# The last block's transposes moved from TensorE to DMA, and the last tile stored in two halves

## Chip, cores, metric

The kernel runs on one core of a Trainium2 chip. The metric is the device time of one execution in microseconds (us); a median is quoted with its lowest and highest run. A ratio between two kernels is the mean time of one kernel's fast runs over the mean of the other's fast runs of the same rounds, so it is not quite the ratio of the medians. A run is called slow when it is over 1.5% above the fastest of the same kernel.

## The reference, cut to what matters

```python
def reference(A_x, A_k_cache, A_v_cache, A_wq, A_wo, B_x, B_w_gate, B_w_up, B_w_down):
    x  = A_x                                   # 2048 x 640, bf16
    xn = layernorm(x)
    s  = attention(xn)      # 32 heads of 192, the last 512 cached keys, then @ wo (6144 x 640)
    g  = silu((silu(xn @ w_gate) * (xn @ w_up)) @ w_down)
    return x + s * g
```

## The kernel before

Heads go in 16 pairs, rows in four blocks of 512, that is 16 tiles of 128 rows. For each pair and block the kernel computes scores, exponentials, `P @ V` (in `pv`), a transpose of the result `O_b` to `OT_b`, and `OT_b @ wo`. The products with `wo` are summed over pairs in `sacc`, already multiplied by `g` and with `x` added. For the last pair, `wo_last` multiplies its product by `g2` (VectorE reads PSUM, writes `s_f`), adds `sacc` (GpSimd or VectorE), and the sum goes to HBM.

Everything that the change touches lies in the last 25 us, where only the last pair is left. `sc_tile()` and `mm_tile()` each rotate over two PSUM buffers. In the cut below, `...` marks what is left out, and the comments are added.

```python
    def pv(i, q2):                       # P @ V of two row tiles, normalised into O_b
        ...
        if (pr == last and b < NB - 1) or i == 0:
            nc.sync.dma_start_transpose(
                out=OT_b[:, 6 * q2 : 6 * q2 + 6, :],
                in_=O_b[:, 2 * q2 : 2 * q2 + 2, :, :].rearrange("p t h d -> p (t h d)"),
            )
        ...
    def transpose_o(i, qt):              # the last block of the last pair only
        trp = psum.tile([P, 3, P], bf, name="trp", tag="mm")
        o_f = Obs[i][:, qt, :, :].rearrange("p h d -> p (h d)")
        for j in range(3):
            nc.tensor.transpose(trp[:, j, :], o_f[:, j * P : (j + 1) * P], ident[:])
        nc.scalar.copy(OTs[i][:, 3 * qt : 3 * qt + 3, :], trp[:, :, :])

    def wo_last(b, qt, eng):
        i, t = last * NB + b, 4 * b + qt
        ob = xrs[t] if b < 2 else finp.tile([P, D], bf, name="ob", bufs=4)
        s_f = finp.tile([P, 2, HD], f32, name="s_f", bufs=3)
        halves = [slice(n * HD, (n + 1) * HD) for n in range(2)]
        split = b == NB - 1 and qt == 3                       # the very last tile
        sc = None if split else sc_tile()
        ps = [(mm_tile()[:, 0, :] if split else sc[:, n, :])[:, 0:HD] for n in range(2)]
        for n, cols in enumerate(halves):
            if late(i):                                       # blocks 2 and 3: 12 matmuls, else 6
                wo_mm(ps[n], i - NB, qt, n, end=False)
            wo_mm(ps[n], i, qt, n, first=not late(i))
            if split:
                nc.vector.tensor_tensor(s_f[:, n, :], ps[n], g2[:, t, cols], ALU.mult)
                nc.vector.tensor_tensor(ob[:, cols], s_f[:, n, :], sacc[:, t, cols], ALU.add)
        if not split:
            nc.vector.tensor_tensor(
                s_f[:], sc[:, :, 0:HD], g2[:, t, :].rearrange("p (n d) -> p n d", n=2), ALU.mult
            )
            eng.tensor_tensor(
                ob[:], s_f[:].rearrange("p n d -> p (n d)"), sacc[:, t, :], ALU.add
            )
        stores.append((t, ob))

    def store(left):                                          # all on SyncE's queue
        while len(stores) > left:
            t, ob = stores.pop(0)
            nc.sync.dma_start(out=out2[t * P : (t + 1) * P, :], in_=ob[:])
    ...
    i = last * NB
    V, G = nc.vector, nc.gpsimd
    for b in range(NB - 1):
        for q2 in range(2):
            pv(i + b, q2)
    for q2 in range(2):
        wo_last(0, 2 * q2, G)
        wo_last(0, 2 * q2 + 1, G)
        pv(i + 3, q2)
    for qt in range(4):                                       # "the loop", four turns
        wo_last(1, qt, G)
        store(3)
        wo_last(2, qt, V if qt % 2 else G)
        transpose_o(i + 3, qt)
    for qt in range(4):                                       # "block 3"
        store(2)
        wo_last(3, qt, V if qt else G)
    store(0)
```

Below, "(2,1)" means block 2, tile 1; its product is s_f(2,1) and its sum ob(2,1).

The softmax here doesn't subtract the row's maximum and nothing guards it: scores larger than these inputs give would overflow.

Of the kernel before, what the change touches and what calls it, by code (L numbers as in the profile page):

```python
# [10 lines left out]
ALU = mybir.AluOpType  # L11
# [4 lines left out]
def kernel(  # L16
# [13 lines left out]
    nc = tc.nc  # L30
    P = nc.NUM_PARTITIONS

    x2 = A_x.flatten_outer_dims()
    out2 = out.flatten_outer_dims()
# [10 lines left out]
    NB = Sq // 512  # L45
# [5 lines left out]
    HD = D // 2  # L51
    scale = float(Dh) ** -0.5
    EPS = 1e-5
    bf = dt.bfloat16
# [14 lines left out]
    psum = ctx.enter_context(tc.tile_pool(name="psum", bufs=2, space=bass.MemoryType.PSUM))  # L69

    def sc_tile():
        return psum.tile([P, 2, 512], f32, name="sc", tag="sc")

    def mm_tile():
        return psum.tile([P, 2, 512], f32, name="mm", tag="mm")
# [5 lines left out]
    g2 = res.tile([P, T, D], bf, name="g2")  # L81


    ident = consts.tile([P, P], bf, name="ident")
# [313 lines left out]
    sacc = sapool.tile([P, T, D], f32, name="sacc")  # L398

    NS = NPAIR * NB  # L400
    last = NPAIR - 1
    Ps, OTs, Obs, xrs = {}, {}, {}, {}
# [32 lines left out]
    def pv(i, q2):  # L435

        pr, b = divmod(i, NB)
        if q2 == 0:
            Obs[i] = opool.tile([P, 4, 2, Dh], bf, name="O_b")
            tag = "OT_l" if late(i) and pr < last else "OT_b"  # L440
            OTs[i] = otpool.tile([P, 12, P], bf, name=tag, tag=tag, bufs=2 if tag == "OT_l" else 3)
        O_b, OT_b = Obs[i], OTs[i]
        alone = i < 2 or (pr == last and b < NB - 1)
        acc = sc_tile() if alone and q2 and b < 2 else mm_tile()
        r = smpool.tile([P, 2, 2, 1], f32, name="r")
        for k in range(2):
            qt = 2 * q2 + k
            for h in range(2):
                for kc in range(KC):
                    nc.tensor.matmul(  # L450
                        acc[:, k, h * 256 : h * 256 + Dh + 1],
                        Ps[i][kc][:, h, qt * P : (qt + 1) * P], V_p[:, kc, h, 0 : Dh + 1],
                        start=(kc == 0), stop=(kc == KC - 1),
                    )
        a_v = acc[:, :, :].rearrange("p k (h c) -> p k h c", h=2)
        nc.vector.reciprocal(r[:], a_v[:, :, :, Dh : Dh + 1])  # L456
        for k in range(2):
            qt = 2 * q2 + k
            a_k = a_v[:, k, :, :]
            if k == 0 and alone:  # L460
                nc.vector.tensor_tensor(
                    O_b[:, qt, :, :], a_k[:, :, 0:Dh], r[:, k, :, :].to_broadcast([P, 2, Dh]),
                    ALU.mult,
                )
                continue
            for h in range(2):
                nc.scalar.activation(  # L467
                    O_b[:, qt, h, :], a_k[:, h, 0:Dh], ACT.Copy, scale=r[:, k, h, :]
                )
        if (pr == last and b < NB - 1) or i == 0:  # L470
            nc.sync.dma_start_transpose(
                out=OT_b[:, 6 * q2 : 6 * q2 + 6, :],
                in_=O_b[:, 2 * q2 : 2 * q2 + 2, :, :].rearrange("p t h d -> p (t h d)"),
            )
        elif pr < last and q2 == 1:
            nc.sync.dma_start_transpose(
                out=OT_b[:, :, :], in_=O_b[:, :, :, :].rearrange("p t h d -> p (t h d)")
            )

    def transpose_o(i, qt):  # L480
        trp = psum.tile([P, 3, P], bf, name="trp", tag="mm")
        o_f = Obs[i][:, qt, :, :].rearrange("p h d -> p (h d)")
        for j in range(3):
            nc.tensor.transpose(trp[:, j, :], o_f[:, j * P : (j + 1) * P], ident[:])
        nc.scalar.copy(OTs[i][:, 3 * qt : 3 * qt + 3, :], trp[:, :, :])

    def load_xr(t):
        xrs[t] = finp.tile([P, D], bf, name="x_r", bufs=8)
# [3 lines left out]
    def late(i):  # L492
        return i // NB >= NPAIR - 2 and i % NB >= 2

    def wo_mm(ps, i, qt, n, first=True, end=True):
        for j in range(3):
            nc.tensor.matmul(  # L497
                ps, OTs[i][:, 3 * qt + j, :], pairs[i // NB]["wo"][:, j, n * HD : (n + 1) * HD],
                start=(first and j == 0), stop=(end and j == 2),
            )  # L500
# [23 lines left out]
# [5 lines that stand above are left out]
        split = b == NB - 1 and qt == 3  # L529
# [3 lines that stand above are left out]
            if late(i):  # L533
                wo_mm(ps[n], i - NB, qt, n, end=False)
            wo_mm(ps[n], i, qt, n, first=not late(i))
            if split:
                nc.vector.tensor_tensor(s_f[:, n, :], ps[n], g2[:, t, cols], ALU.mult)
                nc.vector.tensor_tensor(ob[:, cols], s_f[:, n, :], sacc[:, t, cols], ALU.add)  # L538
        if not split:
            nc.vector.tensor_tensor(  # L540
                s_f[:], sc[:, :, 0:HD], g2[:, t, :].rearrange("p (n d) -> p n d", n=2), ALU.mult
            )
            eng.tensor_tensor(
                ob[:], s_f[:].rearrange("p n d -> p (n d)"), sacc[:, t, :], ALU.add
            )
        stores.append((t, ob))

    def store(left):
# [4 lines that stand above are left out]
    for pr in range(NPAIR):  # L553
        for b in range(NB):
            i = pr * NB + b
# [22 lines left out]
        for b in range(NB):  # L578
            i = pr * NB + b
            for q2 in range(2):  # L580
                pv(i, q2)
                if i >= 2:
                    wo_tile(i - 2, 2 * q2)
                    wo_tile(i - 2, 2 * q2 + 1)
            if b == 0 and pr + 2 < NPAIR:
                load_k(pr + 2)
            elif b == 1 and pr + 2 < NPAIR:
                load_wq(pr + 2)
            elif b == 2:
                load_wo(pr + 1)  # L590
# [9 lines that stand above are left out]
    for qt in range(4):  # L600
        wo_last(1, qt, G)
        store(3)
        wo_last(2, qt, V if qt % 2 else G)
        transpose_o(i + 3, qt)
    for qt in range(4):
        store(2)
        wo_last(3, qt, V if qt else G)
    store(0)


# [28 lines left out]
```

## Time and profile before

The kernel before takes 930.39 us (930.12 to 930.56, 3 runs). Its page gives the busy time of each engine and the chain of work that ended last, by engine:

```profile
PE 920.7 (99%) x8026; PEld 578.7 (62%) x8026; DVE 579.7 (62%) x846; ACT 476.2 (51%) x849; POOL 65.1 (7%) x57
...
PE 98%; DMA 1%; DVE 1%; ACT 0%; issue 0%; SPq 0%; DVEq 0%
```

The same chain in order of time, at the end of the same kernel (columns: start, length, what), seems to agree. It counts each group of three transposes with 0.17 us:

```profile
906.33 2.44 PE sc L497 x18
908.78 0.17 PE trp L484 x3
908.94 0.81 PE sc L497 x6
909.76 0.00 issue
909.76 1.79 PE sc L497 x12
...
917.27 3.27 PE sc L497 x24
...
920.64 0.84 DVE s_f L540
```

The timelines of VectorE and GpSimd in that stretch tell more. First VectorE of the kernel before (start, length, engine, line, operation, out<-in, shapes, number; in brackets the idle time before it and what ended it):

```profile
908.88 0.82 DVE L540 TENSOR_TENSOR s_f<-sc,g_76 128x640 f32<-128x640 f32 x1 [0.81 <-PE sc L497]
...
911.66 0.82 DVE L540 TENSOR_TENSOR s_f<-sc,g_76 128x640 f32<-128x640 f32 x1 [0.97 <-PE sc L497]
912.52 0.99 DVE L543 TENSOR_TENSOR ob<-s_f,sacc 128x640 bf16<-128x640 f32 x1
...
918.07 1.47 DVE L543 TENSOR_TENSOR ob<-s_f,sacc 128x640 bf16<-128x640 f32 x1
919.46 0.81 DVE L540 TENSOR_TENSOR s_f<-sc,g_76 128x640 f32<-128x640 f32 x1
920.64 0.82 DVE L540 TENSOR_TENSOR s_f<-sc,g_76 128x640 f32<-128x640 f32 x1 [0.36 <-PE sc L497]
921.50 1.08 DVE L543 TENSOR_TENSOR ob<-s_f,sacc 128x640 bf16<-128x640 f32 x1
...
923.34 0.83 DVE L543 TENSOR_TENSOR ob<-s_f,sacc 128x640 bf16<-128x640 f32 x1
...
925.53 0.49 DVE L538 TENSOR_TENSOR ob<-s_f,sacc 128x320 bf16<-128x320 f32 x1
```

And GpSimd of the kernel before:

```profile
909.79 1.54 POOL L543 TENSOR_TENSOR ob<-s_f,sacc 128x640 bf16<-128x640 f32 x1
911.29 1.54 POOL L543 TENSOR_TENSOR x_r<-s_f,sacc 128x640 bf16<-128x640 f32 x1
...
917.31 1.55 POOL L543 TENSOR_TENSOR x_r<-s_f,sacc 128x640 bf16<-128x640 f32 x1
920.35 1.54 POOL L543 TENSOR_TENSOR ob<-s_f,sacc 128x640 bf16<-128x640 f32 x1 [1.50 <-DVE s_f L540]
```

The twelve matmuls of block 2 in the chain start at 909.76, 0.06 us after VectorE's multiply of the previous block-2 tile ended (908.88 + 0.82 = 909.70): they wait for one of the two PSUM buffers. And of VectorE's four full-width adds, all of one shape, the last (923.34) runs beside no GpSimd add and takes 0.83 us, while the other three take 0.99, 1.47 and 1.08 us. Each of these three overlaps a GpSimd add, and each ends 0.68 to 0.69 us after that GpSimd add ends: 912.83 to 913.51, 918.86 to 919.54, 921.89 to 922.58.

### The profile page before, as it was taken

Reading aid. Unit: us, or ns where it says so; the run is one execution under the profiler, and the core shown is the slowest. Engines: PE = TensorE matmul, PEld = TensorE weight load, DVE = VectorE, ACT = ScalarE, POOL = GpSimd, SP = SyncE. Lnnn points to the kernel's source line nnn. Section 1 sums busy time; section 2 is a strip of 40 time slices with the busy share of each in tenths; the row PEclk is TensorE's granted clock in tenths of the full one; section 3 lists DMA queues with packets and bytes.
Section 4 is the critical chain, followed back from the end, with each engine's and each line's share of the span. In section 5 each row is a group of like instructions: output and inputs, shape, how many; then the busy total and the mean of one; then the engine's idle time right before and its main releaser. Section 6 shows DMA issues by size and latency. Waiting matters only on the chain.

```text
span 928.8 us, 18808 instructions
## 1 busy us (share of the span) xinstructions
PE 920.7 (99%) x8026; PEld 578.7 (62%) x8026; DVE 579.7 (62%) x846; ACT 476.2 (51%) x849; POOL 65.1 (7%) x57
## 2 busy tenths in 40 slices
PE   8999999999999999999999999999999999999997
PEld 5455555574847475757575757575666666666675
DVE  5433321467676767676766667676767676767656
ACT  3222222556565656565555555555555555656561
POOL 0000000000000000000000000000000000003975
PEclk9999999999999999999999999999999999999999
DMA  9321510053535343343434342525252616262523
GB/s 299 69 43 44 114 35 1 1 80 85 93 71 87 77 80 84 73 91 73 91 69 95 60 104 56 108 52 112 41 123 38 126 35 129 34 144 61 147 59 107
DMA packets 240084, 76.34 MB, mean 82 GB/s; under 512 B 221056, under 2 KB 240000, under 8 KB 240000
## 3 DMA queue, kind: packets, MB, share of 16 engines
q1 hardware_dynamic: 239120, 74.40, 38.1%
q8 instruction: 63, 1.03, 0.5%
q10 hardware_dynamic: 880, 0.74, 0.3%
q14 instruction: 21, 0.17, 0.1%
HBM read 39.45 MB, written 2.62 MB: 45 GB/s over the span
## 4 chain that ended last, share of the span: by engine, by line
PE 98%; DMA 1%; DVE 1%; ACT 0%; issue 0%; SPq 0%; DVEq 0%
PE sc L497 22%; PE mm L414 22%; PE mm L450 18%; PE sc L428 18%; PE sc L271 10%; PE mm L293 6%; DMA x_t<-in_A_x_dram 1%; PE sc L450 1%; PE mm L306 0%; PE mm L271 0%; ACT xnT L321 0%; DVE s_f L540 0%; PE mm L428 0%; ACT L327 0%; DVE ob L538 0%
## 5 line engine op out<-in xcount | busy, mean ns | idle before, releaser
L432 ACT ACTIVATE p_t<-sc 128x1024 bf16<-128x1024 f32 x254 | 253.1, 1023 | 136.4 <-PE sc L428 136.4
L419 DVE TENSOR_REDUCE qT<-mm 128x512 bf16<-128x1024 f32 x189 | 231.3, 1224 | 104.0 <-PE mm L414 101.5
L467 ACT ACTIVATE O_b<-mm,r 128x192 bf16<-128x192 f32 x484 | 164.5, 422 | 175.2 <-DVE r L456 97.6
L414 PE MATMUL mm<-xnT,wq_p 64*128 64x512 bf16 x1890 | 235.0, 376 | 0.0
L497 PE MATMUL sc<-wo_p,OT_b 128*128 128x320 bf16 x1482 | 223.4, 299 | 0.0
L512 DVE TENSOR_TENSOR sacc<-sacc,sc 128x640 f32<-128x640 f32 x216 | 176.7, 821 | 60.9 <-PE sc L497 60.9
L428 PE MATMUL sc<-qT,khat 64*128 64x512 bf16 x1524 | 195.5, 376 | 0.0
L450 PE MATMUL mm<-V_p,p_t 128*128 128x193 bf16 x1984 | 185.8, 246 | 0.0
L450 PEld LDWEIGHTS <-p_t 128*128 128x128 bf16 x2048 | 173.1, 97 | 14.9 <-issue 7.0
L497 PEld LDWEIGHTS <-OT_b 128*128 128x128 bf16 x1488 | 143.5, 98 | 47.3
L414 PEld LDWEIGHTS <-wq_p 64*128 64x128 bf16 x1890 | 90.7, 94 | 112.4 <-issue 4.2
L428 PEld LDWEIGHTS <-khat 64*128 64x128 bf16 x1536 | 74.8, 94 | 91.0
L279 DVE TENSOR_TENSOR hT<-sc,sg 128x512 bf16<-128x512 f32 x46 | 31.7, 692 | 85.8 <-ACT sg L278 85.8
L515 POOL TENSOR_TENSOR sacc<-sacc,g_76 128x640 f32<-128x640 f32 x16 | 22.1, 1402 | 757.8 <-ACT O_b L467 757.8
L456 DVE RECIPROCAL r<-mm 128x4 f32<-128x4 f32 x124 | 22.7, 183 | 73.1 <-PE mm L450 68.9
L278 ACT ACTIVATE sg<-sc 128x512 bf16<-128x512 f32 x46 | 27.4, 597 | 73.2 <-PE sc L271 71.6
L271 PE MATMUL sc<-xnT,wg_sb 128*128 128x512 bf16 (+1 forms) x260 | 58.0, 354 | 1.2 <-ACT xnT L321 0.7
L271 PE MATMUL sc<-xnT,wu_sb 128*128 128x512 bf16 (+1 forms) x260 | 58.2, 354 | 0.0
L293 PE MATMUL mm<-wd_sb,hT 128*128 128x320 bf16 x384 | 56.6, 299 | 0.0
L293 PEld LDWEIGHTS <-hT 128*128 128x128 bf16 x384 | 37.6, 98 | 18.9
L271 PEld LDWEIGHTS <-wu_sb 128*128 128x128 bf16 x285 | 25.8, 98 | 26.5
L271 PEld LDWEIGHTS <-wg_sb 128*128 128x128 bf16 x285 | 25.8, 98 | 24.7 <-DMA wg_sb<-in_B_w_gate_dram 1.1
(63 smaller groups left out, 250.5 us busy)
## 6 DMA issues: line engine op xcount, KB each, us to landing
wo_p<-in_A_wo_dram SPq DMA_DIRECT2D x16, 480.0 KB, 4.3
K_p<-in_A_k_cache_dram SPq DMA_DIRECT2D x32, 192.0 KB, 3.3
V_p<-in_A_v_cache_dram SPq DMA_DIRECT2D x32, 192.0 KB, 3.1
wq_p<-in_A_wq_dram SPq DMA_DIRECT2D x64, 80.0 KB, 3.1
wq_p<-in_A_wq_dram SPq DMA_DIRECT2D x16, 160.0 KB, 3.3
x_r<-in_A_x_dram SPq DMA_DIRECT2D x16, 160.0 KB, 4.1
x_t<-in_A_x_dram SPq DMA_DIRECT2D x14, 160.0 KB, 3.1
wg_sb<-in_B_w_gate_dram SPq DMA_DIRECT2D x4, 480.0 KB, 6.7
```

The costliest lines, as they stand in the source:

```text
L271: nc.tensor.matmul(out, w_sb[:, c, f * P : (f + 1) * P], xnT[:, c, qc], start=(c == 0), stop=(c == NC - 1),)
L278: nc.scalar.activation(sg[:], g, ACT.Silu)
L279: nc.vector.tensor_tensor(hTs[b][:, f, :], u, sg[:], ALU.mult)
L293: nc.tensor.matmul(dn[:, 0:HD], hTs[b][:, f, ti * P : (ti + 1) * P], wd_sb[:, f, cols], start=(f == 0), stop=(f == NF - 1),)
L414: nc.tensor.matmul(q_ps[:, h, :], pairs[pr]["wq"][r, c, j * P : (j + 1) * P], xnT[r, c, b * 512 : (b + 1) * 512], start=(c == 0), stop=(c ...
L419: nc.vector.reduce_sum(qTs[i][:, j, :], q_ps[:, :, :].rearrange("p h n -> p n h"), axis=AX.X)
L428: nc.tensor.matmul(sc[:, h, :], khat[r, j, ks], qT[r, j, :], start=(j == 0), stop=(j == 2))
L432: nc.scalar.activation(p_t[:, :, :], sc[:, :, :], ACT.Exp, scale=scale)
L450: nc.tensor.matmul(acc[:, k, h * 256 : h * 256 + Dh + 1], Ps[i][kc][:, h, qt * P : (qt + 1) * P], V_p[:, kc, h, 0 : Dh + 1], start=(kc == ...
L467: nc.scalar.activation(O_b[:, qt, h, :], a_k[:, h, 0:Dh], ACT.Copy, scale=r[:, k, h, :])
L497: nc.tensor.matmul(ps, OTs[i][:, 3 * qt + j, :], pairs[i // NB]["wo"][:, j, n * HD : (n + 1) * HD], start=(first and j == 0), stop=(end an ...
L512: nc.vector.tensor_tensor(s_t, s_t, sc[:, :, 0:HD], ALU.add)
```

## The change

The intent: take twelve transposes off TensorE, the engine that is 99% busy, by using the DMA transpose that the other blocks use already; and shorten the very last wait by storing the last tile as two halves, the first one early, on two queues. The whole diff:

```diff
--- before.py
+++ after.py
@@ -467,7 +467,7 @@
                 nc.scalar.activation(
                     O_b[:, qt, h, :], a_k[:, h, 0:Dh], ACT.Copy, scale=r[:, k, h, :]
                 )
-        if (pr == last and b < NB - 1) or i == 0:
+        if pr == last or i == 0:
             nc.sync.dma_start_transpose(
                 out=OT_b[:, 6 * q2 : 6 * q2 + 6, :],
                 in_=O_b[:, 2 * q2 : 2 * q2 + 2, :, :].rearrange("p t h d -> p (t h d)"),
@@ -476,13 +476,6 @@
             nc.sync.dma_start_transpose(
                 out=OT_b[:, :, :], in_=O_b[:, :, :, :].rearrange("p t h d -> p (t h d)")
             )
-
-    def transpose_o(i, qt):
-        trp = psum.tile([P, 3, P], bf, name="trp", tag="mm")
-        o_f = Obs[i][:, qt, :, :].rearrange("p h d -> p (h d)")
-        for j in range(3):
-            nc.tensor.transpose(trp[:, j, :], o_f[:, j * P : (j + 1) * P], ident[:])
-        nc.scalar.copy(OTs[i][:, 3 * qt : 3 * qt + 3, :], trp[:, :, :])
 
     def load_xr(t):
         xrs[t] = finp.tile([P, D], bf, name="x_r", bufs=8)
@@ -536,13 +529,15 @@
             if split:
                 nc.vector.tensor_tensor(s_f[:, n, :], ps[n], g2[:, t, cols], ALU.mult)
                 nc.vector.tensor_tensor(ob[:, cols], s_f[:, n, :], sacc[:, t, cols], ALU.add)
-        if not split:
-            nc.vector.tensor_tensor(
-                s_f[:], sc[:, :, 0:HD], g2[:, t, :].rearrange("p (n d) -> p n d", n=2), ALU.mult
-            )
-            eng.tensor_tensor(
-                ob[:], s_f[:].rearrange("p n d -> p (n d)"), sacc[:, t, :], ALU.add
-            )
+                (nc.scalar if n else nc.sync).dma_start(
+                    out=out2[t * P : (t + 1) * P, cols], in_=ob[:, cols]
+                )
+        if split:
+            return
+        nc.vector.tensor_tensor(
+            s_f[:], sc[:, :, 0:HD], g2[:, t, :].rearrange("p (n d) -> p n d", n=2), ALU.mult
+        )
+        eng.tensor_tensor(ob[:], s_f[:].rearrange("p n d -> p (n d)"), sacc[:, t, :], ALU.add)
         stores.append((t, ob))
 
     def store(left):
@@ -601,11 +596,9 @@
         wo_last(1, qt, G)
         store(3)
         wo_last(2, qt, V if qt % 2 else G)
-        transpose_o(i + 3, qt)
     for qt in range(4):
-        store(2)
+        store(2 if qt < 3 else 0)
         wo_last(3, qt, V if qt else G)
-    store(0)
 
 
 # ---- launch: one core; inputs and outputs as the reference has them ----
```

## The prediction

> **What bounds the kernel now.** The page shows TensorE busy 920.7 of 928.8 us at the full granted clock; the chain of waits is TensorE for 98%. The change touches only the last 25 us. There, from 908 us on, the timeline shows something other than the chain suggests: VectorE and GpSimd pace the end.
>
> - In three of the loop's turns block 2's twelve matmuls start 0.06 us after VectorE ends its multiply of the previous such tile (909.70 then 909.76, 912.48 then 912.54, 915.25 then 915.31): they wait for one of two output buffers. A turn takes 2.78 us: 1.79 matmuls, 0.11, 0.82 multiply, 0.06. Matmuls alone need 18 x 0.136 = 2.45, so the transposes (0.17 per turn in the chain) fill a hole that would be a wait.
> - GpSimd's adds take 1.54 us. VectorE's add takes 0.83 alone, but 0.99, 1.47 and 1.08 next to one, ending each time 0.68 us after the GpSimd add (912.83 to 913.51, 918.86 to 919.54, 921.89 to 922.58), whenever it began. The Trainium skill, "SBUF — State Buffer", section "SBUF: two separate sides", says that a VectorE instruction with two SBUF inputs and a GpSimd one reading SBUF exclude each other; this trace agrees. So the end hangs on: block 2's first multiply (908.88, before any transpose), two GpSimd adds (to 912.83), VectorE add, multiply (to 914.25), three GpSimd adds (to 918.86), VectorE add, multiply, GpSimd add (to 921.89), then VectorE without a break to 926.02. No transpose is in that chain.
> - The last store: issued 926.05, packets moving from about 926.9 to 927.5, landing 1.8 us after issue, end at 928.8.
>
> **What the change removes, adds, moves.**
> - Removes 12 TensorE transposes (4 x 0.17 us) and four ScalarE copies of 0.48 us on an idle engine. On the path: about 0. TensorE ends about 0.2 us earlier, but VectorE doesn't wait for it there.
> - Adds two DMA transposes: about 1.23 us of queue time each, 2.8 us to landing. Inputs are ready at about 905.0 and 907.95, so they land near 908 and 911; first use is about 917. They sit ahead of the stores in the same in-order queue, so the first stores slip from 903.8 to about 909.3; at 0.33 us each they catch up by about 912, and no buffer is needed back by then.
> - Splits the last store: only 80 KB remain after 926.02. 1280 B packets took 55 ns; 640 B ones, interpolated between 384 B (22) and 768 B (38), about 32 (estimate). Eight per engine: 0.44 becomes 0.26, about 0.2 us gained. The Trainium skill, "DMA: Bandwidth & Descriptors", section "Issuing engines are not separate DMA queues", says that a second issuing engine saves only issue time; that is 0.33 us here and the halves are 0.9 us apart, so the second queue itself saves little.
>
> **Predicted: 930.2 us** (0.2 less), 80% range 929.5 to 930.8. Faster by over 2%: 0.002; within: 0.996; slower: 0.002.
>
> **What would show it.** Right: a TensorE wait of about 0.17 us where transposes stood; turns still 2.78 us; VectorE's last add still ending near 926.0; the end about 0.2 us nearer to it. Wrong: turns of 2.6 us, VectorE finishing 0.2 to 0.7 us earlier.
>
> **What would make it wrong.** If the chain of waits is right and transposes do cost, up to 0.7 us more is gained. If issue on ScalarE's queue or the final wait for two queues is slower, the store's 0.2 us are lost. If VectorE's add starts ahead of GpSimd's after a shift, the exclusion turns around and the end moves by up to a microsecond. Spread between runs (930.12 to 930.56) is as large as the effect.

## The result

The changed kernel takes 930.49 us (930.07 to 931.72, 6 runs); the kernel before in the same rounds 930.38 us (930.01 to 930.88, 6 runs). The ratio is 1.0003, with a 95% interval of 0.999 to 1.0015. There is no difference that timing can show.

The page of the changed kernel, the lines that answer to those of before:

```profile
PE 919.1 (99%) x7998; PEld 577.8 (62%) x8014; DVE 579.8 (62%) x846; ACT 474.3 (51%) x845; POOL 65.1 (7%) x57
...
PE 97%; DVE 1%; DMA 1%; ACT 0%; issue 0%; SPq 0%; DVEq 0%
```

The profiled spans are 928.83 and 929.62 us, but the 0.79 us between them do not come from the edit. To see this, the span is cut at three marks that both timelines have: the first product of the gate (line 279), VectorE's first reciprocal after the last exponentials, and the end of VectorE's last add. I call the last two pieces T1 and T2.

| piece of the profiled span | before, us | changed, us |
|---|---|---|
| start, to the first product of the gate | 16.76 | 17.37 |
| middle, to the first reciprocal of the last stretch | 876.81 | 877.03 |
| T1, to the end of VectorE's last add | 32.45 | 32.44 |
| T2, to the end of the span | 2.81 | 2.78 |

The start waits for the first loads and differs from run to run (16.49 to 19.90 us over the comparable profiles). The middle's 0.22 us enter at one place, near 206.5 us, where TensorE's weight load waits 0.27 us for an early DMA transpose into `OT_b`, in code that the edit does not touch; the other eleven comparable profiles have middles of 876.81 to 876.93. What the edit touches lies in T1 and T2. Each is read from one profiled execution per kernel; where nothing relevant was changed they repeat to a few hundredths (with one exception, both_sp below). They are the measure in what follows, as the effects are smaller than the spread of whole runs.

VectorE in the changed kernel, the lines that answer to those of before (all starts are 0.83 us later, 894.40 against 893.57 at the mark):

```profile
909.71 1.64 DVE L537 TENSOR_TENSOR s_f<-sc,g_76 128x640 f32<-128x640 f32 x2 [0.81 <-PE sc L490]
912.49 0.82 DVE L537 TENSOR_TENSOR s_f<-sc,g_76 128x640 f32<-128x640 f32 x1 [1.14 <-PE sc L490]
913.35 0.99 DVE L540 TENSOR_TENSOR ob<-s_f,sacc 128x640 bf16<-128x640 f32 x1
...
918.90 1.47 DVE L540 TENSOR_TENSOR ob<-s_f,sacc 128x640 bf16<-128x640 f32 x1
920.28 0.81 DVE L537 TENSOR_TENSOR s_f<-sc,g_76 128x640 f32<-128x640 f32 x1
921.30 0.82 DVE L537 TENSOR_TENSOR s_f<-sc,g_76 128x640 f32<-128x640 f32 x1 [0.20 <-PE sc L490]
922.16 1.24 DVE L540 TENSOR_TENSOR ob<-s_f,sacc 128x640 bf16<-128x640 f32 x1
...
926.35 0.49 DVE L531 TENSOR_TENSOR ob<-s_f,sacc 128x320 bf16<-128x320 f32 x1
```

GpSimd in the changed kernel:

```profile
912.11 1.54 POOL L540 TENSOR_TENSOR x_r<-s_f,sacc 128x640 bf16<-128x640 f32 x1
...
918.14 1.53 POOL L540 TENSOR_TENSOR x_r<-s_f,sacc 128x640 bf16<-128x640 f32 x1
921.17 1.54 POOL L540 TENSOR_TENSOR ob<-s_f,sacc 128x640 bf16<-128x640 f32 x1 [1.50 <-DVE s_f L537]
```

And TensorE in the changed kernel, where the transposes stood:

```profile
909.03 1.39 PE L490 MATMUL sc<-wo_p,OT_b 128*128 128x320 bf16 x9
910.59 0.57 PE L490 MATMUL sc<-wo_p,OT_l 128*128 128x320 bf16 x3 [0.17 <-DVE s_f L537]
...
911.81 1.39 PE L490 MATMUL sc<-wo_p,OT_b 128*128 128x320 bf16 x9
913.36 0.57 PE L490 MATMUL sc<-wo_p,OT_l 128*128 128x320 bf16 x3 [0.17 <-DVE s_f L537]
```

The transposes' 0.17 us turned into a wait of 0.17 us for VectorE, which the brackets now name. A turn of the loop is still 913.36 - 910.59 = 2.77 us. The chain of the changed kernel shows the same with VectorE pieces in it, which the chain of before did not have:

```profile
909.71 0.83 DVE s_f L537
910.55 0.04 issue
910.59 1.80 PE sc L490 x12
```

After the last group TensorE is really 0.17 us ahead, and s_f(3,1) starts 0.17 us earlier against the mark (921.30 - 894.40 = 26.90, before 920.64 - 893.57 = 27.07). The add behind it then takes 1.24 us instead of 1.08 and ends 922.16 + 1.24 - 922.71 = 0.69 us after GpSimd's add, as before. This is where the gain of the transposes ends.

For T2, the trace's records of packets and semaphores give five steps. "Exit" is all that comes after the last landing.

| T2, us | issue | to first packet | packets | to last landing | exit | sum |
|---|---|---|---|---|---|---|
| before (160 KB, SyncE) | 0.027 | 0.835 | 0.596 | 0.342 | 1.011 | 2.811 |
| changed (last 80 KB, ScalarE) | 0.031 | 0.864 | 0.417 | 0.371 | 1.094 | 2.777 |

The packets take 0.18 us less, and the other steps take 0.145 us more. The largest of these is the exit. There SyncE waits in a fixed order for all DMA completion semaphores, and for some of the engines': seven rows of one or two, about 0.06 us from one to the next. The DMAs take eight semaphores in rotation, whatever queue they are on. Before, the last store's semaphore stood in the third row, with four rows behind it. The change adds three DMAs (two transposes, one store more), and the last store falls on the first semaphore of the second row, with five rows behind it. That is 0.06 us; another 0.02 us pass in the row itself (0.078 us from the landing to the start of the next row, before 0.059).

### The profile page after: what moved, and what is told of

Read it like the earlier page. It is cut to its first block, busy times and chain, and to the rows that moved or that the text cites. A ratio compares the mean times of both kernels' runs of the same rounds, so it can differ in the third digit from the quotient of the medians.

```text
span 929.6 us, 18769 instructions
## 1 busy us (share of the span) xinstructions
PE 919.1 (99%) x7998; PEld 577.8 (62%) x8014; DVE 579.8 (62%) x846; ACT 474.3 (51%) x845; POOL 65.1 (7%) x57
## 4 chain that ended last, share of the span: by engine, by line
PE 97%; DVE 1%; DMA 1%; ACT 0%; issue 0%; SPq 0%; DVEq 0%
PE mm L414 22%; PE sc L490 22%; PE mm L450 18%; PE sc L428 18%; PE sc L271 10%; PE mm L293 6%; DMA x_t<-in_A_x_dram 1%; PE sc L450 1%; DVE s_f L537 0%; PE mm L306 0%; PE mm L271 0%; ACT xnT L321 0%; PE mm L428 0%; ACT L327 0%; DVE ob L531 0%
```

## Experiments

The theory: VectorE and GpSimd pace the end, since a VectorE add with two SBUF inputs cannot run beside a GpSimd add; TensorE waits for PSUM buffers, so its transposes cost nothing; and the store's gain is lost around the packets. The rival takes the chain of waits at its word: TensorE paces, so the transposes cost 4 x 0.17 = 0.67 us, and a halved store gains its whole transfer time.

| kernel | median us (range, runs) | before, same rounds | ratio (95%) | T1 | T2 |
|---|---|---|---|---|---|
| t_only | 932.42 (930.47 to 933.88, 4) | 930.49 | 1.0016 (1.0 to 1.0032) | 32.45 | 2.93 |
| t_only2, the same again | 930.92 (930.51 to 931.43, 4) | 930.59 | 0.9997 (0.9981 to 1.0012) | 32.44 | 2.94 |
| split_only | 930.53 (930.2 to 931.35, 4) | 930.49 | 0.9998 (0.9983 to 1.0013) | 32.45 | 2.76 |
| both_sp | 930.55 (930.21 to 930.94, 4) | 930.49 | 0.9997 (0.998 to 1.0014) | 32.44 | 2.89 |
| trp_double | 930.39 (930.11 to 930.57, 4) | 930.49 | 0.9995 (0.998 to 1.001) | 32.46 | 2.80 |
| nolock_pe | 930.7 (930.09 to 931.47, 4) | 930.71 | 0.9996 (0.9981 to 1.0011) | 32.23 | 2.81 |
| nolock_dma2 | 930.19 (929.98 to 930.64, 4) | 930.59 | 0.9991 (0.9977 to 1.0005) | 32.08 | 2.77 |
| nolock_dma (its 3 fast runs) | 929.78 (929.75 to 930.12, 3) | 930.71 | 0.9988 (0.9972 to 1.0003) | - | - |
| lane_shift | 930.59 (930.32 to 930.85, 4) | 930.71 | 0.9995 (0.9982 to 1.0009) | 32.45 | 2.51 |
| best | 928.86 (928.27 to 929.26, 5) | 930.71 | 0.9976 (0.9964 to 0.9989) | 30.24 | 3.24 |
| best2 | 928.2 (928.07 to 928.71, 5) | 930.59 | 0.997 (0.9958 to 0.9983) | 30.24 | 2.74 |

All gave correct results. None differs from the kernel before by 2%; only for best and best2 does the interval lie wholly below 1. nolock_dma had one slow execution, the profiled one, so it has no T1 and T2; it is told below.

### t_only and t_only2: the transposes alone

```diff
-        if (pr == last and b < NB - 1) or i == 0:
+        if pr == last or i == 0:
...
-        transpose_o(i + 3, qt)
```

> Only the transposes move to DMA; the last store stays whole. Two lengths are read from the profile: T1, from the start of VectorE's first reciprocal of the last stretch (the one that comes right after the last exponentials) to the end of VectorE's last add (before 32.45 us, changed kernel 32.44), and T2, from there to the end of the span (before 2.81, changed 2.78). My theory (VectorE and GpSimd pace the end, transposes fill a hole): T1 stays within 0.03 of 32.45. Rival, the chain of waits taken at its word (TensorE paces, transposes cost 4 x 0.17): T1 about 31.8. For T2 I expect 2.93: the exit waits for each DMA completion semaphore in a fixed order, 0.06 us a row, and two more DMAs put the last store on a semaphore that stands two rows earlier; a theory without that says 2.81.

T1 was 32.45 and T2 2.93, both as expected; moving the transposes gains nothing. The 0.12 us more of T2 are all in the exit (1.133 us against 1.011): two DMAs more put the last store on the semaphore of the first row, with six rows behind it instead of four. The whole was 1.9 us slower in the median, however, which I had not expected. The profiled run had lost 3.1 us at the start, by the first gate product (19.90 instead of 16.76 us), in loads that the edit does not touch.

> The kernel t_only again, because three of its four executions were 1.5 to 3.4 us slower than before although T1 was 32.45; the profiled one lost 3.1 us by the first gated product at the kernel's start (19.9 instead of 16.8 us), in loads that the edit doesn't touch. If that is chance, the median comes back to within 0.5 us of before, with T1 32.45 and T2 2.93 again. If it belongs to this program, the start is late again.

In this second run, on another chip, the first gate product came at 17.45 us, the median was 0.33 us over before with a ratio of 0.9997, and T1 and T2 repeated (32.44 and 2.94). The late start did not come back, so nothing ties it to the edit. Why three of four executions of the first run were slower is open (only the profiled one is known to have started late); of seven executions of the kernel before in those rounds one was over 931.5 us.

### trp_double: twice as many transposes on TensorE

```diff
-        for j in range(3):
+        for j in (0, 1, 2, 0, 1, 2):
             nc.tensor.transpose(trp[:, j, :], o_f[:, j * P : (j + 1) * P], ident[:])
```

> The kernel before, with each TensorE transpose made twice (the same result written again; 12 more, 0.17 us more per group of three). My theory: the hole of 0.17 us in each turn takes them, and after the last group VectorE's add still ends by GpSimd's end: T1 32.45 within 0.05. Rival (TensorE paces): T1 grows by 4 x 0.17 to about 33.1.

T1 was 32.46, the same within 0.01 us: twelve transposes more cost nothing, where the rival asked for 0.67. There was room for them. A turn of 2.78 us holds 2.45 us of matmuls at full pace (18 x 0.136) and 0.33 us more, which is two groups of transposes; before, one group filled half of it. In the profile of this kernel, TensorE makes six transposes where it made three:

```profile
908.57 0.50 PE L484 MATMUL trp<-ident,O_b 128*128 128x128 bf16 x6
908.84 0.82 DVE L540 TENSOR_TENSOR s_f<-sc,g 128x640 f32<-128x640 f32 x1 [0.81 <-PE sc L497]
908.90 0.98 PE L497 MATMUL sc<-wo_p,OT_b 128*128 128x320 bf16 x6
...
909.72 0.57 PE L497 MATMUL sc<-wo_p,OT_l 128*128 128x320 bf16 x3
```

Block 2's matmuls start at 909.72, still 0.06 us after VectorE's multiply (908.84 + 0.82 = 909.66). VectorE's timeline of the same kernel shows the end of the stretch:

```profile
920.77 0.82 DVE L540 TENSOR_TENSOR s_f<-sc,g 128x640 f32<-128x640 f32 x1 [0.54 <-PE sc L497]
921.63 0.90 DVE L543 TENSOR_TENSOR ob<-s_f,sacc 128x640 bf16<-128x640 f32 x1
```

The multiply comes 0.17 us later than before against the same mark, and the add behind it takes 0.90 us instead of 1.08, ending 0.68 us after GpSimd's add (920.31 + 1.54 = 921.85). Its start moved and its end did not. The rival falls with this run.

### nolock_pe, nolock_dma and nolock_dma2: the exclusion taken away

The product that VectorE adds itself beside a GpSimd add is written to a free PSUM buffer. VectorE's add then has one SBUF input. The edit was made in the kernel before (nolock_pe) and in the changed kernel (nolock_dma).

```diff
-        s_f = finp.tile([P, 2, HD], f32, name="s_f", bufs=3)
+        psum_sum = (b, qt) in ((2, 1), (2, 3), (3, 1))
+        s_f = (
+            mm_tile()[:, :, 0:HD] if psum_sum else finp.tile([P, 2, HD], f32, name="s_f", bufs=3)[:]
+        )
...
```

> The same edit in the kernel before, with the transposes on TensorE. My theory: T1 falls from 32.45 to about 32.25 only, so about 0.17 to 0.20 us longer than the same edit with DMA transposes: that is the one group of transposes (of four) that no other wait hides. If transposes cost nothing even then, both have the same T1; if all four cost, the difference is 0.67.

> The changed kernel; the three products that VectorE later adds beside GpSimd are written to PSUM, not SBUF, so that VectorE's add has one SBUF input. My theory (GpSimd shuts out VectorE's add, and the transposes' time shows once that is gone): the adds beside GpSimd take 0.83 to 0.9 us instead of 0.99, 1.47 and 1.24; T1 falls from 32.44 to about 32.05, where TensorE paces. Rival (adds are slow for another cause, or TensorE paced all along): T1 stays 32.44.

> The same kernel as nolock_dma, whose profiled execution fell in a state with a granted clock of 0.75 and can't be compared. Expected again, at full clock: T1 about 32.05, some 0.17 to 0.20 us under the 32.23 measured for the same edit with TensorE transposes. Rival (the transposes cost nothing even without the exclusion): 32.23.

The profiled execution of nolock_dma: granted clock 0.753 and a span of 1203.3 us, while its three others took 929.75 to 930.12 us. The kernel was run again as nolock_dma2. With TensorE transposes T1 was 32.23, with DMA transposes 32.08. The adds in nolock_dma2, on VectorE:

```profile
912.97 0.82 DVE L543 TENSOR_TENSOR ob<-mm,sacc 128x640 bf16<-128x640 f32 x1
...
918.53 0.82 DVE L543 TENSOR_TENSOR ob<-mm,sacc 128x640 bf16<-128x640 f32 x1
...
921.72 0.82 DVE L543 TENSOR_TENSOR ob<-mm,sacc 128x640 bf16<-128x640 f32 x1
```

All three take 0.82 us, though GpSimd adds in part of the time of at least two of them (its adds started at 911.73, 917.60 and 920.19, of 1.53 to 1.54 us each). So the long adds came from the exclusion (the third add hardly meets GpSimd's here, 921.72 against 921.73, and shows nothing either way); this agrees with the Trainium skill, "SBUF — State Buffer", section "Who interferes with whom", which says that a VectorE instruction with at most one SBUF input outside the 2-port modes does not contend with GpSimd. And once the exclusion is gone, the DMA transposes are worth 32.23 - 32.08 = 0.15 us. That is about one group of the four (0.17); the other three still hide behind the wait for a PSUM buffer.

### split_only and both_sp: the store

split_only is the kernel before with the change's split store:

```diff
                 nc.vector.tensor_tensor(ob[:, cols], s_f[:, n, :], sacc[:, t, cols], ALU.add)
+                (nc.scalar if n else nc.sync).dma_start(
+                    out=out2[t * P : (t + 1) * P, cols], in_=ob[:, cols]
+                )
...
```

> Transposes on TensorE as before, only the last tile stored as two halves on two queues. My theory: T1 32.45 as before; T2 2.76 to 2.81, although the packets of the last store take 0.42 instead of 0.60 us: 0.03 lost before the first packet, 0.03 at the landing, and about 0.06 in the exit's row of waits. Rival (the halved store gains its full transfer time): T2 2.63.

T2 was 2.76, in the expected range. both_sp is the changed kernel with `nc.sync` for both halves.

> The changed kernel with both halves issued by SyncE instead of one by ScalarE. If ScalarE's queue costs something, the time from VectorE's last add to the first packet of the last store falls from 0.895 (changed) to about 0.86 as before, and T2 from 2.78 to about 2.75. If the queue makes no difference T2 stays 2.78. If the second queue helps, T2 grows above 2.80. T1 32.44 in each case.

This one came out half right. From issue to the first packet it took 0.823 us instead of 0.864, so ScalarE's queue costs 0.04 us there. But T2 grew to 2.89 instead of falling to 2.75, as the exit took 1.239 us. The rows of semaphore waits were the same as in the changed kernel; what was late was TensorE's last drain, 0.894 us after the landing instead of 0.708. Without it T2 would have been about 2.75 us (an estimate: 2.89 less the 0.145 us by which this exit is longer than the changed kernel's), which is what was expected if ScalarE's queue costs something. One run shows the late drain, and its cause is open.

| T2, us | issue | to first packet | packets | to last landing | exit | rows behind the last store's |
|---|---|---|---|---|---|---|
| t_only | 0.027 | 0.831 | 0.597 | 0.342 | 1.133 | 6 |
| split_only | 0.031 | 0.869 | 0.423 | 0.363 | 1.072 | 5 |
| both_sp | 0.027 | 0.823 | 0.417 | 0.386 | 1.239 | 5 |
| lane_shift | 0.032 | 0.864 | 0.422 | 0.361 | 0.834 | 1 |

### lane_shift: the last store on the semaphore waited for last

Four loads of `x` tiles, some 90 us before the end, become two half loads each, which turns the rotation of semaphores by four.

```diff
-        nc.sync.dma_start(out=xrs[t][:], in_=x2[t * P : (t + 1) * P, :])
+        for c in (slice(0, HD), slice(HD, D)) if 8 <= t < 12 else (slice(0, D),):
+            nc.sync.dma_start(out=xrs[t][:, c], in_=x2[t * P : (t + 1) * P, c])
```

> The changed kernel with four loads in mid-kernel issued as two halves each, so that four DMAs more are counted and the last store falls on the completion semaphore that the exit waits for last. My theory: the time from the landing of the last store to the end falls from 1.09 (changed) to about 0.85, T2 from 2.78 to about 2.53; T1 stays 32.44. Rival (the order of the exit's waits doesn't matter): T2 2.78.

The exit fell to 0.834 us and T2 to 2.51, with T1 unmoved. Four DMAs more, at about 835 us, made the end 0.26 us shorter, more than the split store alone gained (0.05). What the four do plays no part in it; their number turns the rotation.

### best and best2: a version that beats both

The DMA transposes leave two PSUM buffers free (`mm`). Block 2's tiles take them, so that no turn waits for a buffer. VectorE multiplies in place in PSUM where it adds itself. Block 3's adds alternate. The loads of lane_shift are in it too.

```diff
-        sc = None if split else sc_tile()
+        sc = None if split else mm_tile() if b == 2 else sc_tile()
...
+        elif eng is V:
+            s_ps = sc[:, :, 0:HD]
+        else:
+            s_ps = finp.tile([P, 2, HD], f32, name="s_f", bufs=4)[:]
...
-        wo_last(3, qt, V if qt else G)
+        wo_last(3, qt, V if qt % 2 else G)
```

In best both last halves go out on SyncE, in best2 on ScalarE.

> All findings together on the changed kernel: block 2's tiles use the PSUM buffers that the transposes left free, so TensorE waits for no buffer (a turn 2.45 instead of 2.78 us); VectorE's products stay in PSUM where it adds them itself; the last block's adds alternate between GpSimd and VectorE; both last halves on SyncE's queue; and the last store on the semaphore waited for last. My theory: T1 about 30.3 (2.1 less), T2 about 2.5, the whole about 2.4 us (0.26%) under before at an equal start. If TensorE's buffers were not the limit, T1 stays above 31.5.

> The combined kernel with both last halves issued by ScalarE. In the combined kernel before it the end of VectorE's work moved by 2.2 us (T1 30.24) but 0.7 us were lost after it, as the last stores stood in SyncE's in-order queue behind a store that waited for GpSimd. Theory: with a queue of their own they go out 0.03 us after their data, T2 falls from 3.24 to about 2.5, T1 stays 30.24; at an equal start the whole is about 2.5 us (0.27%) under before. If the store engines and not the queue held them back, T2 stays above 3.

T1 fell to 30.24 in both, as expected. T2 did not come out as expected in either. In best it was 3.24: the last store was issued 0.72 us after its data was ready, since SyncE's queue works in order: it stood waiting for GpSimd's ob(3,2) until 923.39, and then issued that store and the first half (ready since 922.67) before the last one (ready at 923.60). In best2 the last halves had a queue of their own and went out after 0.03 us, but from the issue of the last half to its last packet it took 1.51 us instead of 0.864 + 0.417 = 1.28 in the changed kernel, as their packets shared the DMA engines with the whole tile of ob(3,2); T2 was 2.74, not 2.5. This is what the Trainium skill says in "DMA: Bandwidth & Descriptors", section "Issuing engines are not separate DMA queues": all queues run on the same DMA engines. The chain of best2 shows the loop now:

```profile
908.61 0.81 PE sc L491 x6
909.42 1.63 PE mm L491 x12
911.05 0.81 PE sc L491 x6
911.87 1.63 PE mm L491 x12
...
920.94 0.82 DVE s_f L543
```

A turn is 911.87 - 909.42 = 2.45 us, the 18 matmuls alone. Of the 2.20 us that T1 is shorter than in the changed kernel, 1.06 come before the product s_f(3,1) (26.90 us after the mark in the changed kernel, 25.84 in best2), about 1.0 of it from three turns at 0.33 us less. The other 1.14 come after it, where GpSimd adds (3,2) and VectorE's add of (3,1) takes 0.82 us instead of 1.24. best2 takes 928.2 us, a ratio of 0.997 (0.9958 to 0.9983) to before. It is not shown that this needs the DMA transposes: nolock_pe used `mm` buffers for three products beside TensorE transposes, and no run gave block 2 the `mm` buffers with the transposes left on TensorE.

## Why the prediction was right

- **TensorE waits for PSUM buffers, a turn stays 2.78 us: right.** The changed kernel shows the predicted wait of 0.17 us where the transposes stood, and turns of 2.77 us; trp_double put twelve more transposes in and moved T1 by 0.00 us; best2, with block 2 in two other buffers, runs a turn in 2.45 us.
- **VectorE's adds end by GpSimd's end: right.** The three adds end 0.68 to 0.70 us after GpSimd's in both kernels. The 0.17 us that TensorE did gain were swallowed in one of them (1.24 instead of 1.08 us). Taking the exclusion away brought all three to 0.82 us and let 0.15 us of the transposes' time appear. The predicted chain leaves out that VectorE does wait for TensorE once there, before s_f(3,1) (0.36 us before, 0.20 in the changed kernel); the earlier product gained nothing because the add behind it ended by GpSimd's end.
- **DMA transposes in time, stores catch up: right.** Against the mark they landed at 907.8 and 910.7 on the clock of before (predicted 908 and 911), and the first store went out at 909.2 (predicted 909.3).
- **The store's gain of 0.2 us: mis-sized.** The step was "Eight per engine: 0.44 becomes 0.26, about 0.2 us gained", with the sign "the end about 0.2 us nearer to it". The packets did take 0.18 us less (0.596 to 0.417), and T2 fell by only 0.034. I took the rest of T2 as fixed; the risk that the gain is lost was named, but for "the final wait for two queues", and what moved the exit was the number of DMAs. It grew by 0.145: 0.03 until the first packet (both_sp took that back by using SyncE's queue), 0.03 until the landing, and 0.083 in the exit. For the exit, t_only and lane_shift show that the place of the last store's semaphore in the order of waits decides, with about 0.06 us a row.
- **The time: right, but it could not test much.** 930.49 was measured for 930.2; the part that was predicted as a gain is smaller than the spread of runs (930.07 to 931.72). Of the predicted gain of 0.2 us, T1 and T2 together show 0.04, and the medians differ by 0.11 us the other way; that the time fell into the range is no evidence for the store's step, as a forecast of no change would have done as well. The pieces T1 and T2 are what supports the argument, not the median.

## What to carry to other kernels

A chain of waits that names the busiest engine is not proof that this engine paces a stretch: look whether its instructions start a fixed few hundredths after another engine's end, and put the suspected cost in twice to see whether the end moves. When an engine's time is removed, ask what will hold its next instruction; here it was a PSUM buffer in three turns of four, and the turns became shorter only in the runs that gave block 2 other buffers. For the last microseconds, cut the time after the last compute instruction into issue, first packet, packets, landing and exit, since a gain in one is easily lost in another, and compare such pieces rather than whole runs when the start varies more than the effect.

## What the Trainium skill lacked or had wrong

- "SBUF — State Buffer", section "SBUF: two separate sides", says that the loser of the shared ports fully blocks. The trace agrees in the main and is a little more exact: an add of 0.82 to 0.83 us ended 0.68 to 0.70 us after the GpSimd add, whenever it had begun, so about 0.14 us of the two records overlap. Whether the add does any work in that time they do not tell.
- No page that I found tells that the end of a program waits for every DMA completion semaphore in a fixed order. Here it cost about 0.06 us a row, and the exit was 0.834 to 1.147 us long for one to six rows behind the last store's (both_sp, 1.239, had another delay besides).
- "DMA: Bandwidth & Descriptors", section "Latency and other measured facts", gives about 0.6 us to the first byte for SyncE's and ScalarE's DMAs, and does not say from when. From the start of the issuing instruction to the first packet it was 0.82 to 0.84 us on SyncE and 0.86 to 0.87 on ScalarE, of which the instruction itself took 0.33 and 0.36 to 0.37; from its end it was about 0.5.
- The same page, section "Issuing engines are not separate DMA queues", says that a second issuing engine only saves the time of issuing. It can save more: in best the first half was ready at 922.67 us and went out on SyncE at 923.84, 1.17 us later, as the queue works in order and stood before a store whose data came at 923.39. In best2, on ScalarE, the first half went out 0.03 us after its data. For the last half the second engine saved 0.69 us of waiting, of which about 0.2 were given back by sharing the DMA engines.
